# A convolution and an attention on one core: one pool of four PSUM tiles in the last quarter, in place of three tiles in turn

## The chip, the cores and the metric

The kernel runs on one core of one Trainium2 chip. The metric is device time in microseconds (us), the median of several executions. Engines are called as in the profile: PE (matmuls), PEld (PE's weight loads), DVE, ACT, POOL, and SP, which issues all the DMAs. PSUM is the memory that PE writes into and that DVE and ACT read; it holds eight tiles of 128 x 512 f32 here, one to a bank, and all eight are given away at any time.

## What is computed

Two independent results stand side by side in the output. Columns 0 to 447 are a long convolution of `A_u` (2048 x 448) with a kernel made from the `A_` parameters; columns 448 to 895 are attention with 16 heads of 28 over `B_x` (2048 x 448).

```python
K = 2.0 * jnp.einsum("dn,dnl->dl", C, exp((A * dt)[:, :, None] * pos)).real     # 448 x 2048, 256 terms each
a = irfft(rfft(u_t, 2 * L) * rfft(K, 2 * L), 2 * L)[:, :, :L] + u * D_skip
qkv = x @ wqkv
b = softmax(q k^T * Dh**-0.5) v, heads joined, @ wo
out = concatenate([a, b], axis=-1)
```

## The kernel before, in words

The first stage (lines 206 to 540) projects q, k and v, makes the seeds of the convolution's powers and the row maxima of the first unit of attention. Here the order on the engines is the planner's. From line 846 on every instruction keeps the order of the program on its engine, SP's DMAs too.

The main loop (lines 978 to 1030) has 256 steps. A unit `u` is a group of 4 heads and a chunk of 512 queries; it has 16 steps `kt`, one for each 128 keys. `ORDER` (line 33) is the order of a step: `m0 s0 m1 s1 v f pv f v m2 s2 m3 s3 v`.

- `s0` to `s3` are the scores of four heads (`s_mm`, line 698): a matmul into `pss` (a pool of three) and the exponential `p` on ACT. `pv` (line 705) multiplies the p of the step before by v, into `po`.
- `m0` to `m3` are the row maxima that a later unit will need, 19 steps ahead (`max_mm`, line 167). Each is a matmul into a working tile. For `m0` ACT reads the tile (`rl`, a Relu); for `m1` DVE's custom instruction joins it to that `rl`; for `m2` and `m3` DVE reduces it to `mx`. They end when 19 steps are left.
- `v` is a part of the convolution kernel's powers on DVE (`g`, with the factors in the PSUM tile `zg` of pool `ps_g`); POOL does another part (`e`).
- `f` calls `slot` (line 934), which runs the next small task that is due, if any: `sums`, `scale` and `project` of a finished unit (lines 726 to 753), the transform of u, the matmuls of the convolution kernel's blocks (`k_mm`), and then the jobs of the spectrum and of the output (`f_slot`).

A **spectrum job** (`spectrum`, line 760; 16 of them) has four tasks. `forth(0)` and `last` each run 8 matmuls `pm<-yk,mw` into a working tile (x16 in the trace, which counts two instructions for each), and DVE multiplies it by u's spectrum twice (`pr`, line 781). `last` then does both `join`s: DVE makes one half of `p0` and of `p1`, POOL the other (lines 786, 787). After a gap of two slots `back(0)` and `back(1)` run matmuls `pm<-p,mw` into a working tile each, and ACT copies it out (`y`). An **output job** (`finish`, line 803; 8 of them) has four tasks: matmuls `pm<-zi,wb`, and DVE adds `ut`, which POOL has multiplied (`ot`, line 836).

All these working tiles come from `w_tile` (line 124). It has three names, `pm0`, `pm1`, `pm2`, one tile each in pool `ps_m`, and takes them strictly in turn. A matmul that takes a tile waits until the tile's last reader has finished. So PSUM in the main loop is: `ps_m` 3, `pss` 3, `po` 1, `zg` 1.

The factors' tile `zg` is last needed when the convolution kernel's last block is done. Line 986 notes that point (step 192 or later, nothing left in `k_due`, `m_due`, `powers`), closes the pool of the blocks' SBUF tiles, and lets the second half of the spectrum jobs begin. In the trace the last use of `zg` lies at 1060 us and the last of the blocks' matmuls at 1076 us of the span, so line 986 acts at about 1079 us.

Of the kernel before, what the change touches and what calls it, by code (L numbers as in the profile page):

```python
# [7 lines left out]
F32 = mybir.dt.float32  # L8
# [5 lines left out]
PSUM = bass.MemoryType.PSUM  # L14
# [9 lines left out]
CQ = 512  # L24
# [64 lines left out]
def body(ctx, tc, a, out):  # L89
# [5 lines left out]
    def pool(stack, name, bufs=1, space=None, side=None):  # L95
        kw = {} if space is None else {"space": space}
        if side:
            kw["side"] = side
        return stack.enter_context(tc.tile_pool(name=name, bufs=bufs, reuse_waits="tile", **kw))
# [18 lines left out]
    w1 = const.tile([128, 2, 128], F32, name="w1")  # L118

    att, k0_st = ExitStack(), ExitStack()  # L120
    ps_m = pool(att, "ps_m", 1, PSUM)
    n_ring = [0]

    def w_tile():

        n_ring[0] += 1
        return ps_m.tile([128, CQ], F32, name=f"pm{n_ring[0] % 3}")

    q_p = pool(att, "q_p", side="right")
    v_p = pool(att, "v_p", side="right")  # L130
# [10 lines left out]
    def load_k(g, j, p):  # L141
        t = p.tile([128, L], F32R, name="khat", bufs=HG)
        for r in range(4):
            nc.sync.dma_start(t[32 * r:32 * r + 32, :].bitcast(F32), k_d[g][r % 2, 32 * j:32 * j + 32, :])
        kt_g.setdefault(g, []).append(t)
# [3 lines left out]
    def load_v(g, c):  # L149
        v_g[g, c] = t = v_p.tile([128, NK // NQ, HG, 32], F32, name="v", bufs=5)  # L150
        nc.sync.dma_start(t.rearrange("p t h e -> p t (h e)"), v_d[c][:, g])
# [3 lines left out]
    def load_kd(g, j):  # L155
        kd_g[g, j] = t = kd_p[0].tile([128, CQ], F32R, name=f"kdif{j}")
        for r in range(4):
            nc.sync.dma_start(t[32 * r:32 * r + 32].bitcast(F32), kd_d[g][r % 2, 32 * j:32 * j + 32, :])

    def load_q(u):  # L160
        g, c = divmod(u, NQ)
        t = q_p.tile([128, HG, CQ], F32R, name="qhat", bufs=3)
        for r in range(4):
            nc.sync.dma_start(t[32 * r:32 * r + 32].bitcast(F32), q_d[g][c][r // 2].rearrange("(j p) q -> p j q", j=HG))
        q_u[u] = t

    def max_mm(u, i, kc, ps=w_tile):

        if i == 0 and kc == 0:
            m_u[u] = q_p.tile([128, HG, 4, 3], F32, name="mx", bufs=2)  # L170
        j, t = divmod(i, 4)
        pm = ps()
        q, kt = q_u[u][:, j, t * 128:(t + 1) * 128], kt_g[u // NQ][j]
        mx = m_u[u][:, j, t, max(kc - 1, 0):max(kc - 1, 0) + 1]
        if kc == 0:
            nc.tensor.matmul(pm, q, kd_g[u // NQ, j], start=True, stop=True)
            rl_u[u, i] = kd_p[0].tile([128, CQ], F32, name="rl", bufs=2)
            nc.scalar.activation(rl_u[u, i], pm, AF.Relu)
        elif kc == 1:
            kb = kt.rearrange("p (c s n) -> p c s n", c=NQ, s=2)[:, :2, 1, :]  # L180
            nc.tensor.matmul(pm.rearrange("p (c n) -> p c n", c=2), q, kb, start=True, stop=True)
            rl = rl_u.pop((u, i))
            nc.vector.tensor_tensor_reduce(rl, pm, rl, 1.0, -3.0e38, ALU.add, ALU.max, mx)
        else:
            nc.tensor.matmul(pm, q, kt[:, kc * CQ:(kc + 1) * CQ], start=True, stop=True)
            nc.vector.tensor_reduce(mx, pm, axis=AX.X, op=ALU.max)
# [19 lines left out]
    with ExitStack() as st:  # L206
# [3 lines left out]
        x_p = pool(xst, "x_p")  # L210
        y_p = pool(wst, "y_p", side="right")
        w_p = pool(wst, "w_p", side="right")
        ps_t = pool(st, "ps_t", 2, PSUM)
        ps_n = pool(st, "ps_n", 2, PSUM)
        ps_x = pool(st, "ps_x", 1, PSUM)
# [223 lines left out]

        def qk_proj(c, s, g):  # L440
            pp = w_tile()
            hs = slice(HG * g, HG * g + HG)
            n = 0
# [99 lines left out]
    kq_st = ExitStack()  # L543
# [2 lines left out]
    g_p = pool(g_st, "g_p")  # L546
    ps_s = pool(att, "ps_s", 3, PSUM)
    ps_o = pool(att, "ps_o", 1, PSUM)
    ps_g = pool(att, "ps_g", 1, PSUM)
    k_pools = [k0_p, kq_p]  # L550

    late = [False]
# [145 lines left out]
    def s_mm(u, kt, j):  # L698
        pss = ps_s.tile([128, CQ], F32, name="pss")
        nc.tensor.matmul(pss, kt_g[u // NQ][j][:, kt * 128:(kt + 1) * 128], q_u[u][:, j, :], start=True, stop=True)  # L700
        p = kq_p.tile([128, CQ], F32, name="p", bufs=PB)
        nc.scalar.activation(p, pss, AF.Exp, scale=SCALE)
        return p

    def pv_step(u, kt, ps):
        if kt == 0:
            o_u[u] = ps_o.tile([128, CQ], F32, name="po")
        for j in range(HG):
            nc.tensor.matmul(o_u[u][32 * j:32 * j + 32, :], v_g[u // NQ, kt // NQ][:, kt % NQ, j, :], ps[j],
                             start=kt == 0, stop=kt == NK - 1, tile_position=(0, 32 * j))  # L710
# [3 lines left out]
    def load_og(u):  # L714
        og_u[u] = og = kq_p.tile([128, G - 1, CQ], F32, name="og")
        nc.sync.dma_start(og, on_d[u % NQ][:G - 1].rearrange("g p q -> p g q"))
# [169 lines left out]
    f0_st, f1_st = ExitStack(), ExitStack()  # L886
# [47 lines left out]
    def slot(s_):  # L934
        n_slot[0] += 1
        if urgent and urgent[0][0] <= n_slot[0]:
            urgent.popleft()[2]()
        elif s_ >= NS and f_slot(s_, "s"):
            pass
        elif p_due and p_due[0][0] <= s_:  # L940
            p_due.popleft()[1]()
        elif m_due and m_due[0][0] <= s_:
            m_due.popleft()[1]()
        elif u_due and u_due[0][0] <= s_:
            u_part(*u_due.popleft()[1:])
        else:
            f_slot(s_, "s") or f_slot(s_, "f")

    def k_begin(s_):
        if not (k_due and K0 + k_due[0] * KP <= s_ and done["mm"] >= k_due[0] - 2 and not powers["e"] and not powers["g"]):  # L950
            return
        b = k_due.popleft()
        k_start(b)
        powers["g"] += g_powers(b)
        powers["e"] += [lambda i=i, q=q: e_power(b, i, q) for i in range(3) for q in range(3)]
        p0, p1, p2 = k_mm(b)

        def m1():
            p1()
            done["mm"] = b  # L960
        m_due.extend((s_ + KD, t_) for t_ in (p0, m1, p2))
        last[0] = b
# [10 lines left out]
    def vec():  # L973
        if powers["g"]:
            powers["g"].popleft()()

    prev = None
    for s in range(NS):
        u, kt = divmod(s, NK)
        sm = s + NK + LEAD  # L980
        k_begin(s)
        if s == 12 * NK:
            k0_st.close()
            f_p["s", 0] = f_p["s", 1] = pool(f0_st, "f0_p", side="right")
            f_ready["s", 0], f_ready["s", 1] = s, NS
        if s >= 12 * NK and f_ready["s", 1] == NS and not (k_due or m_due or powers["g"] or powers["e"]):
            g_st.close()
            f_ready["s", 1] = s + F1
        if kt == 12 and u // NQ == G - 1:
            load_og(u)  # L990
        late[0] = s + NK + LEAD > NS
        if u % NQ == NQ - 1 and u < NU - 1 and kt % 4 == 2:
            load_v(u // NQ + 1, kt // 4)
        if sm < NS and sm // NK % NQ == NQ - 1 and sm % NK % 4 == 0 and sm % NK and sm // (NQ * NK) + 1 < G:
            load_kd(sm // (NQ * NK) + 1, sm % NK // 4 - 1)
        if sm < NS and sm % (NQ * NK) == 0 and sm:
            load_kd(sm // (NQ * NK), HG - 1)
        if kt % 4 == 1 and u % NQ == 1 and u // NQ + 1 < G:
            load_k(u // NQ + 1, kt // 4, k_pools[(u // NQ + 1) % 2])
        if kt == 2:  # L1000
            if u + 2 < NU:
                load_q(u + 2)
        for _ in range(3):
            if powers["e"]:
                powers["e"].popleft()()
        ps = []
        for op in ORDER:
            if op[0] == "s":
                ps.append(s_mm(u, kt, int(op[1])))
            elif op[0] == "f":  # L1010
                slot(s)
            elif op[0] == "v":
                vec()
            elif op == "pv":
                if prev:
                    pv_step(*prev)
                    if prev[1] == NK - 1:
                        fin(prev[0], s)
            elif sm < NS:
                max_mm(sm // NK, sm % NK, int(op[1]))  # L1020
        for _ in range(FX if late[0] else 0):
            slot(s)
        if sm < NS and sm % NK == NK - 1:
            def end(un=sm // NK):
                max_end(un, w_tile())
                max_put(un)
            max_join(sm // NK)
            soon_slot(UG[0], end)
        k_next()
        prev = (u, kt, ps)  # L1030
# [4 lines left out]
        slot(s)  # L1035
        s += 0.5
    assert not k_due and not powers["g"] and not powers["e"]
    for st in (f1_st, kq_st, f0_st, att):
        st.close()


# [55 lines left out]
```

## Time and profile before

| | us |
|---|---|
| median of 3 runs (1426.0 to 1428.26) | 1427.25 |
| the profiled execution | 1427.0 |
| its span, first to last instruction | 1425.2 |
| span from 1079.5 to 1341.5 (after line 986 acts, until the spectrum jobs are nearly done) | 262.0 |
| span from 1341.5 to 1404 (output jobs, attention without maxima) | 62.5 |
| span from 1404 to the end | 21.2 |

The profile and its trace are of one execution; the 1.8 us between its time and its span lie outside the instructions. PEclk is the clock that PE was granted, as a part of full speed. A row of the timeline gives start, length, engine, line, operation, out<-in, shapes and the number of instructions merged, and in brackets how long the engine sat idle before it, and for what. Line 73 is that of a helper which records every instruction, so tiles tell the groups apart, not lines. A matmul's length is modelled and overlaps the next one's start.

### The profile page before, as it was taken

The numbers are of one execution on the slowest core, as the hardware profiler recorded it, in microseconds if no ns is written. First come the engines' busy times: TensorE is split into PE (matmuls) and PEld (weight loads), VectorE is DVE, ScalarE is ACT, GpSimd is POOL, SyncE is SP. The second block draws the span as 40 slices with busy tenths as digits, with TensorE's granted clock in tenths as the row PEclk, the third lists the DMA queues.
The fourth block names the chain that finished last, engine by engine and source line by source line (L and its number), as shares of the span: only waits on it lengthen the run. The fifth ranks groups of instructions, "written<-read, shape, count | busy, mean of one in ns | idle before, by whom it ended". The sixth has DMA issues, their size and how long they took to land.

```text
span 1425.2 us, 33209 instructions
## 1 busy us (share of the span) xinstructions
PE 1273.5 (89%) x12625; PEld 707.7 (50%) x12625; DVE 978.6 (69%) x2138; ACT 974.4 (68%) x2069; POOL 830.8 (58%) x705
## 2 busy tenths in 40 slices
PE   6978856899999999999999999999988898898998
PEld 4756633445555555555555555555544444433433
DVE  5688766877778777777777878877786646645411
ACT  5867642688788888888787877878775545544553
POOL 3657650587778787778878878887861101102211
PEclk9998887899999999999999999999999999998999
DMA  6666679447663654586441316333244334435476
GB/s 190 236 235 216 225 267 249 112 98 180 150 149 85 152 151 122 157 200 165 140 91 40 92 36 150 89 79 84 55 136 134 112 106 144 154 110 164 134 199 175
DMA packets 200729, 205.37 MB, mean 144 GB/s; under 512 B 96632, under 2 KB 159160, under 8 KB 198520
## 3 DMA queue, kind: packets, MB, share of 16 engines
q1 hardware_dynamic: 200568, 203.23, 51.4%
q8 instruction: 100, 1.64, 0.5%
q14 instruction: 61, 0.50, 0.1%
HBM read 120.73 MB, written 82.18 MB: 142 GB/s over the span
## 4 chain that ended last, share of the span: by engine, by line
PE 58%; DVE 23%; ACT 7%; POOL 6%; issue 3%; DMA 3%; SPq 0%; ACTq 0%; DVEq 0%; POOLq 0%
PE pm L73 34%; PE po L73 13%; PE pss L73 11%; DVE mx L73 5%; DVE g L73 4%; DVE rl L73 3%; DVE p L73 3%; POOL qhat L73 3%; ACT p L73 2%; DVE pr L73 2%; ACT rl L73 2%; DVE tri L73 1%; DVE px L73 1%; DVE zg L73 1%; POOL x_e L73 1%
## 5 line engine op out<-in xcount | busy, mean ns | idle before, releaser
L73 ACT ACTIVATE p<-pss 128x512 f32<-128x512 f32 x1024 | 563.0, 607 | 162.4 <-PE pss L73 153.4
L73 DVE TENSOR_REDUCE mx<-pm 128x1 f32<-128x512 f32 x500 | 321.3, 683 | 141.5 <-PE pm L73 140.6
L73 PE MATMUL pss<-qhat,khat 128*128 128x512 f32 x1024 | 405.2, 402 | 3.2 <-ACT p L73 3.2
L73 PE MATMUL pm<-khat,qhat 128*128 128x512 f32 x749 | 335.3, 451 | 62.0 <-DVE mx L73 60.2
L73 POOL TENSOR_TENSOR e<-e,sdb 128x256 f32<-128x256 f32 x168 | 201.6, 1200 | 185.2 <-ACT e L73 129.6
L73 PE MATMUL po<-p,v 128*32 128x512 f32 x2048 | 278.8, 612 | 0.0
L73 PEld LDWEIGHTS pm<-khat,qhat 128*128 128x128 f32 x749 | 142.4, 190 | 247.3 <-DVE mx L73 114.9
L73 POOL TENSOR_TENSOR e<-e,eu 128x256 f32<-128x256 f32 x168 | 248.3, 1478 | 13.2
L73 DVE CUSTOM_DVE_ANT_0 rl<-pm,rl 128x512 f32<-128x512 f32 x249 | 171.5, 689 | 107.2 <-ACT rl L73 86.9
L73 PEld LDWEIGHTS pss<-qhat,khat 128*128 128x128 f32 x1024 | 192.0, 190 | 46.1 <-ACT p L73 12.8
L73 POOL TENSOR_TENSOR eu<-e,sdb 128x256 f32<-128x256 f32 x168 | 201.9, 1202 | 0.0
L73 POOL TENSOR_TENSOR p<-pr,pr 64x448 f32<-64x448 f32 x32 | 40.6, 1269 | 237.5 <-DVE pr L73 236.3
L73 ACT ACTIVATE rl<-pm 128x512 f32<-128x512 f32 x249 | 150.2, 603 | 32.3 <-PE pm L73 31.6
L73 DVE TENSOR_TENSOR g<-g,zg 128x128 f32<-128x128 f32 x392 | 162.7, 415 | 5.0
L73 PE MATMUL pm<-kdif,qhat 128*128 128x512 f32 x249 | 103.7, 417 | 14.9 <-DVE ot L73 4.0
L73 PEld LDWEIGHTS pm<-e,g 128*32 128x32 f32 x3584 | 64.0, 110 | 52.2 <-issue 34.2
L73 DVE TENSOR_TENSOR zg<-g,zg 128x128 f32<-128x128 f32 x224 | 87.3, 390 | 3.5
L73 ACT ACTIVATE y<-pm 128x448 f32<-128x448 f32 x48 | 26.3, 549 | 80.4 <-PE pm L73 54.1
L73 PEld LDWEIGHTS po<-p,v 128*32 128x32 f32 x2048 | 57.5, 111 | 43.8 <-issue 39.1
L73 PE MATMUL pm<-e,g 128*32 128x64 f32 x3584 | 72.8, 220 | 0.0
L73 PEld LDWEIGHTS pm<-kdif,qhat 128*128 128x128 f32 x249 | 47.3, 190 | 43.5 <-PE pss L73 9.7
L73 PE MATMUL pm<-xh,wh 112*128 112x512 f32 x128 | 54.5, 430 | 13.5 <-DVE tl L73 6.3
(137 smaller groups left out, 1545.8 us busy)
## 6 DMA issues: line engine op xcount, KB each, us to landing
sdb<-sd SPq DMA_DIRECT2D x56, 336.0 KB
qhat<-q SPq DMA_DIRECT2D x64, 256.0 KB
khat<-k SPq DMA_DIRECT2D x64, 256.0 KB
sd<-sg SPq DMA_DIRECT2D x8, 1456.0 KB
mw<-in_mw SPq DMA_DIRECT2D x16, 512.0 KB
sd<-qhat SPq DMA_DIRECT2D x8, 896.0 KB
yk<-yk SPq DMA_DIRECT2D x56, 128.0 KB
yu_d<-ub SPq DMA_DIRECT2D x64, 112.0 KB
```

What stands on the lines that cost most here:

```text
L73: i = f(*args, **kw)
```

## The change

`w_tile` now takes its pool and its number of names from `ps_w`. The three names of the first stage come from a pool `ps_w` that closes with that stage; the main loop gets a new pool `ps_m` with the same three names. When line 986's condition holds, `ps_g` and `ps_m` are closed and a pool `ps_f` is opened over their four banks. It has one name and four buffers; from there on a working tile is any of the four that the pool hands out, not the next in a fixed turn.

```diff
-    ps_m = pool(att, "ps_m", 1, PSUM)
-    n_ring = [0]
+    ps_w, n_ring = [None, 3], [0]
...
         n_ring[0] += 1
-        return ps_m.tile([128, CQ], F32, name=f"pm{n_ring[0] % 3}")
+        return ps_w[0].tile([128, CQ], F32, name=f"pm{n_ring[0] % ps_w[1]}")
...
+        ps_w[0] = pool(st, "ps_w", 1, PSUM)
...
-    ps_g = pool(att, "ps_g", 1, PSUM)
+    ps_st = ExitStack()
+    ps_g = pool(ps_st, "ps_g", 1, PSUM)
+    ps_w[0] = pool(ps_st, "ps_m", 1, PSUM)
...
             g_st.close()
+            ps_st.close()
+            ps_w[:] = pool(ps_st, "ps_f", 4, PSUM), 1
```

More of the change, by code (lines that the diff above doesn't have):

```diff
@@ L1037, in body @@
     assert not k_due and not powers["g"] and not powers["e"]
-    for st in (f1_st, kq_st, f0_st, att):
+    for st in (ps_st, f1_st, kq_st, f0_st, att):
         st.close()
```

## The prediction

> **What bounds the kernel now.** I looked first at where PE is busy and at what clock, because the change can act only after line 986: in the page's slices (PE and PEclk), then in a table by stage.
>
> ```profile
> PE   6978856899999999999999999999988898898998
> PEclk9998887899999999999999999999999999998999
> DMA  6666679447663654586441316333244334435476
> 1079.50:1341.50 262.00, 224.96 (x2044) 108.17 (x2042) 151.74 (x257) 128.43 (x244) 41.30 (x32) 0.92 0.42 137
> 1341.50:1404.00 62.50, 59.05 (x554) 22.32 (x554) 8.68 (x22) 36.13 (x69) 11.98 (x6) 1.00 0.71 189
> 1404.00:1425.20 21.20, 15.96 (x216) 6.65 (x216) 3.73 (x9) 2.38 (x5) 2.10 (x1) 0.98 0.50 135
> ```
>
> The columns of the table are the stretch and its length, then the busy time of PE, PEld, DVE, ACT and POOL, the granted clock, the DMA share and GB/s. In the 262 us after line 986 PE is busy 225 us, more than any other engine; it loses 37.0 us in idling and works at a clock of 0.92, so about 0.08 x 262 = 21 us more go in slow matmuls. Behind 1341.5 PE is nearly full at clock 1.00, and maxima and joins are over: little is to be had there. So at most some 58 us stand to be won. Next, the waits of PE in that stretch (total, times, longest):
>
> ```profile
> PE pm L73 <- DVE mx L73: 24.0, 10, 2.5
> PE pm L73 <- DVE ot L73: 5.0, 2, 4.0
> PE pm L73 <- DVE pr L73: 3.2, 13, 0.3
> PE pm L73 <- DVE mh L73: 2.4, 1, 2.4
> PE pm L73 <- DVE p L73: 1.5, 2, 0.9
> ```
>
> All but the last row are waits for a working tile that DVE hasn't read yet; the last is for an operand. Ten stalls of 2.4 us on the maxima carry it. The timeline of one such stall says why:
>
> ```profile
> 1196.06 0.94 PE L73 MATMUL pm<-yk,mw 128*32 128x224 f32 x16
> 1196.93 0.50 PE L73 MATMUL pm<-khat,qhat 128*128 128x512 f32 x1
> 1197.06 1.16 DVE L73 TENSOR_TENSOR pr<-pm,ub 128x448 f32<-128x448 f32 x2 [0.46 <-PE pm L73]
> 1197.49 0.39 PE L73 MATMUL pm<-khat,qhat 128*128 128x512 f32 x1
> 1198.25 2.67 DVE L73 TENSOR_TENSOR p<-pr,pr 64x448 f32<-64x448 f32 x2
> 1198.37 0.47 PE L73 MATMUL pm<-kdif,qhat 128*128 128x512 f32 x1 [0.26 <-DVE pr L73]
> 1198.68 0.40 PE L73 MATMUL pss<-qhat,khat 128*128 128x512 f32 x1
> 1198.87 0.60 ACT L73 ACTIVATE rl<-pm 128x512 f32<-128x512 f32 x1
> 1200.85 1.28 DVE L73 TENSOR_REDUCE mx<-pm 128x1 f32<-128x512 f32 x2
> 1201.58 0.50 PE L73 MATMUL pm<-khat,qhat 128*128 128x512 f32 x1 [2.51 <-DVE mx L73]
> 1201.92 0.40 PE L73 MATMUL pss<-qhat,khat 128*128 128x512 f32 x1
> 1202.25 1.85 PE L73 MATMUL po<-p,v 128*32 128x512 f32 x8
> 1203.85 1.74 PE L73 MATMUL pm<-p,mw 128*32 128x224 f32 x16
> ```
>
> `last` (1196.06) is followed on PE by m2 (1196.93) and m3 (1197.49), and on DVE by two `pr`, then both joins (2.67 us, needing no PSUM at all), and only then by the reduces of m2 and m3 (1200.85). The next step's m0 (1198.37) takes the tile of `last`; its m1 takes, by turn, the tile of m2, and stands until 1201.58. PE idles 2.51 us. Note the `rl` at 1198.87: ACT has read m0's tile by 1199.47, two microseconds before m1 gets its own, but the turn doesn't give that tile out.
>
> **The stall also closes the clock.** Slicing the span at the points where the clock changes gives steps of 3.41 us:
>
> ```profile
> 1065.86:1069.28 3.42, 1.94 (x22) 0.87 (x26) 2.72 (x5) 0.60 (x1) 0.34 (x1) 1.00 0.00 0
> 1103.41:1106.82 3.41, 1.77 (x22) 1.11 (x26) 2.88 (x5) 1.38 (x4) 0.50 (x1) 1.00 0.22 80
> 1106.82:1110.24 3.42, 3.42 (x32) 2.05 (x24) 1.43 (x3) 2.20 (x5) 0.00 (x0) 1.00 0.30 100
> 1117.06:1120.48 3.42, 1.26 (x5) 0.48 (x3) 3.31 (x4) 1.87 (x4) 1.57 (x2) 1.00 0.00 0
> 1120.48:1123.89 3.41, 3.41 (x29) 1.52 (x32) 0.70 (x2) 1.14 (x2) 0.00 (x0) 0.50 0.04 13
> ```
>
> A step in which PE idles 3.42 - 1.26 = 2.16 us is followed by one at half clock (1117.06, then 0.50 at 1120.48); a step with 3.41 - 1.77 = 1.64 us idle (1103.41) is not (1106.82, at 1.00). So here the point lies between 1.64 and 2.16 us of idling inside one step. What a half-clock step costs, from two stretches with the same work (m1, s1, back, pv, back, up to m2), one without it and one with it:
>
> ```profile
> 1105.05 0.50 PE L73 MATMUL pm<-khat,qhat 128*128 128x512 f32 x1 [2.15 <-DVE mx L73]
> 1108.25 0.50 PE L73 MATMUL pm<-khat,qhat 128*128 128x512 f32 x1
> 1119.85 0.50 PE L73 MATMUL pm<-khat,qhat 128*128 128x512 f32 x1 [2.15 <-DVE mx L73]
> 1124.67 0.50 PE L73 MATMUL pm<-khat,qhat 128*128 128x512 f32 x1
> ```
>
> 3.20 us against 4.82 us: 1.62 us each. The 21 us above are thus 13 such steps.
>
> **The change, part by part.** It adds no instruction and takes none away; every engine keeps its order, and SP's DMAs theirs. The first stage keeps three names and the main loop starts with three, in other banks; the first maxima of the main loop find banks that nobody uses, so nothing is queued there, and I cost that part at nothing (both ends within 1 us: the largest wait it could move is one reduce, 0.64 us of the 1.28 us row). The switch itself gives out banks whose readers finished long ago (`zg`) or one step ago: at most the two reduces of one step, 1.28 us, once; I take nothing.
>
> What is left is which tile a matmul waits for. Four tiles in a fixed turn would move the wait on m2's reduce by one tile, from m1 to `back(0)`. But a pool with several buffers doesn't take turns: it gives out whichever comes free first in the planner's order. The built program of the kernel before shows it in its two-tile pool `ps_t`, in the maxima of the first unit: three times a tile read by ACT's `rl` alone is given out again at once, while the other, waiting for a DVE reduce, is passed over. So `back(0)` should get m0's tile, free after the `rl`.
>
> Worked on the stall above, where PE takes 0.34 us for a full-width matmul after a halt (1201.58 to 1201.92) and 0.22 to 0.23 for the next (1196.93 to 1197.49 is 0.56 for both), 0.86 for a pv, and the first join 1.20, both by the chain that ended last:
>
> ```profile
> 1195.38 0.86 PE po L73 x8
> 1198.25 1.20 DVE p L73
> ```
>
> m0 would start at 1197.94, m1 at 1198.40 (it gets the tile of `last`, whose `pr` ends at 1198.22), s1, pv at 1198.96, `back(0)` at 1199.82. Its operand p0 is the first join, done at 1198.25 + 1.20 = 1199.45. It ends at 1200.9. Now m2 needs a tile: m2's old one at about 1201.5 (the end of the first of the two reduces), or that of `back(0)` after ACT's copy, about the same. **What is late next is thus m2, by some 0.65 us**, in place of 2.51. Where a small task stands between m1 and pv (three of the ten) it takes m0's tile in the same way, and the wait left is no longer in sum; I take the same. That is seven stalls of this form: 7 x (2.5 - 0.65) = 13.0 us.
>
> The other three of the ten have `last` ahead of pv, and the stall comes a step later:
>
> ```profile
> 1184.94 0.40 PE L73 MATMUL pss<-qhat,khat 128*128 128x512 f32 x1
> 1185.48 0.60 ACT L73 ACTIVATE rl<-pm 128x512 f32<-128x512 f32 x1
> 1187.48 0.50 PE L73 MATMUL pm<-khat,qhat 128*128 128x512 f32 x1 [2.14 <-DVE mx L73]
> ```
>
> There m1 and s1 run on at 1185.2, `back(0)` wants its tile at 1185.73 and gets m0's at 1186.08: 0.3 us are left, and pv then covers the reduce. 3 x (2.15 - 0.3) = 5.5 us.
>
> The small waits on `pr` (3.2 us, 13 times) fall with the fourth tile, since m0 needn't take the tile just multiplied: 3.0 us. At the one stall on `mh` the tiles of `last`, `mh`, m2 and m3 are all behind the joins; only m0 and its `rl` get ahead: 2.4 becomes 1.8, 0.6 us. At the 4.0 us stall on `ot` DVE itself waits for POOL, behind POOL's share of the joins; two matmuls get ahead, 0.8 us; the other `ot` wait goes whole, 1.0 us.
>
> Sum of the idling: 13.0 + 5.5 + 3.0 + 0.6 + 0.8 + 1.0 = 24 us of the 37.
>
> With single waits of 0.3 and 0.65 us no step idles 1.64 us any more, so the clock stays open, but for the `ot` stall and perhaps the `mh` one: two half-clock steps of 13 stay. 11 x 1.62 = 18 us.
>
> Hidden cost: DVE must now do its work in 262 - 42 = 220 us; it is busy 152 us there, ACT 128, and both wait on PE after each stall today. The DMA share of 0.42 becomes 0.5; the page's first seven slices stand at 0.6 to 0.9. The next job's loads are issued one job ahead. I count nothing for these.
>
> 1427.0 - 24 - 18 = **1385 us** for the profiled execution; it stands 0.25 us under the median, which I leave out.
>
> **The bounds.** If every wait but those on an operand went and the clock stayed open: 37.0 - 1.5 + 21 = 56.5 us, 1370.5. From the other side, see the rivals.
>
> **The rivals.** (1) *The turn stays.* If the planner gives the four out as a ring, `back(0)` waits for m2's reduce. In the seven-stall form without a small task (four) that leaves 1201.58 - 1200.0 = 1.58 us, counting m1, s1 and pv run meanwhile as won; PE then reaches `back(0)` 1.54 us sooner (0.34 + 0.34 + 0.86). In the three others of that form, and in the form with `last` ahead of pv, only m1 and s1 get ahead, 0.68 us each. 4 x 1.54 + 6 x 0.68 + 2 for the rest = 12 us; seven of the stalls are then near 1.6 us, about the longest that left the clock open: 7 x 1.62 = 11 us. 1427 - 23 = 1404. For it: a plan is not the chip. Against it: m0's `rl` is done 2 us ahead of m2's reduce in the trace, a wide margin for a plan to miss.
>
> (2) *The clock closes all the same*, since a job still has several short waits in one step: 1427 - 24 = 1403. Against it: steps with 1.48 us idle (1065.86, row above) and 1.64 us stayed open. [...]
>
> (3) *The stall only moves*, since DVE's joins stay in front of the reduces: each stall saves what one score matmul and one maximum cover, 0.46 us, 12 x 0.46 = 6, and some of the clock, 5: 1416.
>
> (4) *No change:* another thing ends last in every job, and the won time is given back at the next wait. [...] Here 35 us of waits carry the name of a PSUM tile, which speaks against it.
>
> (5) *Slower:* the plan misjudges the joins and gives m0, not m1, the tile whose reduce lies behind them. Then m0 and s0 lose the cover that they have today, 0.56 us at each of 12 stalls: 1427 + 6.7 = 1434. It decides if the plan has DVE through 2.67 us of joins and one reduce within the 0.7 us that PE takes from m2 to m0. That is unlikely.
>
> **Chances.** Forecast 1385: 0.50. Rivals 1 and 2 together, 1403 to 1404: 0.27. Rival 3, 1416: 0.10. No change: 0.06. Slower, 1434: 0.07. The range reaches down to that bound and the rivals 1 and 2 with some margin: 1371 to 1414. A difference under 0.2% (2.9 us) can't be told from none. Faster 0.87, same 0.06, slower 0.07.
>
> **What would show it.** In the profile after: PEclk of 0.98 to 1.00 in the stage behind line 986; PE's waits on `mx` from 24 us to below 9; m1 at most 0.3 us behind m0's pair after each join; DVE's and ACT's busy times as before. If instead `back(0)` waits for `mx` for 1.6 us, rival 1 holds; if the idling falls and the clock doesn't rise, rival 2. I am wrong altogether if PE waits at m0, or if a wait on a DMA or on ACT takes the place of the one on `mx`.

## The result and the profile after

The changed kernel takes 1383.35 us (median of 4, 1381.05 to 1385.67) against 1426.62 for the kernel before beside it (median of 4, 1424.25 to 1428.26): a ratio of 0.9698, 95% interval 0.9682 to 0.9714, or 43 us less. The profiled execution has a span of 1381.8 us, 43.4 less than before.

These are the rows of PE and of its clock on the page in 40 slices, of the kernel after:

```profile
PE   6977874899999999999999998999999999998997
PEclk9989996899999999999999999999999999999999
```

From slice 31 on the clock stands at 9 throughout, where before it had one 8: a tenth is too coarse. PE's row, which had an 8 in six of these ten slices, has one, and a 7 at the very end. The table by stage says more. Its stretches are the same pieces of work as those of the kernel before (each ends at the same matmuls), and its columns are the same: the stretch and its length, the busy time of PE, PEld, DVE, ACT and POOL, the granted clock, the DMA share and GB/s.

```profile
1081.60:1298.30 216.70, 201.57 (x2044) 104.51 (x2042) 150.27 (x257) 125.70 (x244) 41.61 (x32) 0.99 0.51 166
1298.30:1360.70 62.40, 59.05 (x554) 22.35 (x554) 8.67 (x22) 36.04 (x69) 11.92 (x6) 1.00 0.71 191
1360.70:1381.80 21.10, 15.76 (x216) 6.79 (x216) 3.72 (x9) 2.42 (x5) 2.11 (x1) 1.00 0.48 129
```

The stage behind line 986 shrank from 262.0 to 216.7 us, with the same numbers of matmuls (x2044) and nearly the same busy time on DVE, ACT and POOL. The other two stretches did not move. Of the 45.3 us, PE's idling gave 37.0 - 15.1 = 21.9 and PE's busy time 225.0 - 201.6 = 23.4, at a clock of 0.99 in place of 0.92. What PE still waits for in that stretch (total, times, longest):

```profile
PE pm L73 <- DVE mx L73: 4.7, 6, 0.9
PE pm L73 <- DVE ot L73: 3.5, 1, 3.5
PE pm L73 <- ACT rl L73: 1.9, 4, 0.8
PE pm L73 <- DVE p L73: 1.5, 2, 0.9
```

The 24.0 us on `mx` have become 4.7, and there is no row for `pr` any more. The timeline of the first pair of joins behind line 986 shows the new order of waits:

```profile
1083.71 0.94 PE L73 MATMUL pm<-yk,mw 128*32 128x224 f32 x16
1085.61 0.40 PE L73 MATMUL pm<-kdif,qhat 128*128 128x512 f32 x1
1085.91 2.69 DVE L73 TENSOR_TENSOR p<-pr,pr 64x448 f32<-64x448 f32 x2
1086.08 0.41 PE L73 MATMUL pm<-khat,qhat 128*128 128x512 f32 x1
1086.38 0.61 ACT L73 ACTIVATE rl<-pm 128x512 f32<-128x512 f32 x1
1086.66 1.07 PE L73 MATMUL po<-p,v 128*32 128x512 f32 x8
1087.54 0.94 PE L73 MATMUL pm<-p,mw 128*32 128x224 f32 x16
1088.53 1.27 DVE L73 TENSOR_REDUCE mx<-pm 128x1 f32<-128x512 f32 x2
1089.26 0.50 PE L73 MATMUL pm<-khat,qhat 128*128 128x512 f32 x1 [0.78 <-DVE mx L73]
```

m1 (1086.08) runs right behind m0's pair, and `back(0)` (1087.54) runs a microsecond ahead of the reduce that it would have had to wait for in a fixed turn. What is late next is m2, by 0.78 us. One long stall is left, at the output job's `ot`; there the clock closes once:

```profile
1190.70:1194.12 3.42, 1.87 (x20) 0.94 (x22) 3.37 (x6) 2.25 (x5) 1.49 (x2) 1.00 0.81 269
1248.73:1252.14 3.41, 1.03 (x10) 0.59 (x14) 1.48 (x3) 0.37 (x2) 1.90 (x1) 1.00 0.86 202
1252.14:1255.56 3.42, 3.42 (x35) 1.44 (x28) 0.71 (x3) 0.87 (x2) 0.00 (x0) 0.50 0.20 67
```

In this trace, from 290 us on, the clock changes only at the ends of steps of 3.41 us. The step with 3.41 - 1.03 = 2.38 us idle is followed by one at 0.50. Of the other steps in this stage the one that idled most, 3.42 - 1.87 = 1.55 us, is not.

### The profile page after: what moved, and what is told of

Its sections match the earlier page's. It is cut to its first block, busy times and chain, and to the rows that moved or that the text cites. A ratio compares the mean times of both kernels' runs of the same rounds, so it can differ in the third digit from the quotient of the medians.

```text
span 1381.8 us, 33199 instructions
## 1 busy us (share of the span) xinstructions
PE 1254.3 (91%) x12625; PEld 707.4 (51%) x12625; DVE 979.4 (71%) x2138; ACT 971.6 (70%) x2069; POOL 830.7 (60%) x705
## 3 DMA queue, kind: packets, MB, share of 16 engines
q8 instruction: 100, 1.64, 0.5%
## 4 chain that ended last, share of the span: by engine, by line
PE 58%; DVE 23%; ACT 7%; POOL 5%; issue 3%; DMA 2%; SPq 0%; ACTq 0%; DVEq 0%; POOLq 0%
PE pm L73 34%; PE po L73 13%; PE pss L73 11%; DVE mx L73 6%; DVE g L73 4%; DVE rl L73 3%; POOL qhat L73 3%; ACT p L73 2%; DVE p L73 2%; ACT rl L73 2%; DVE tri L73 1%; DVE pr L73 1%; DVE px L73 1%; DVE sg L73 1%; DVE zg L73 1%
## 5 line engine op out<-in xcount | busy, mean ns | idle before, releaser
L73 PE MATMUL pm<-khat,qhat 128*128 128x512 f32 x749 | 333.9, 449 | 45.3 <-DVE mx L73 39.6
L73 POOL TENSOR_TENSOR e<-e,sdb 128x256 f32<-128x256 f32 x168 | 201.6, 1200 | 185.5 <-ACT e L73 129.7
L73 PE MATMUL po<-p,v 128*32 128x512 f32 x2048 | 272.2, 599 | 0.0
L73 PEld LDWEIGHTS pss<-qhat,khat 128*128 128x128 f32 x1024 | 191.3, 189 | 47.2 <-ACT p L73 12.9
```

The costliest lines, as they stand in the source:

```text
L73: i = f(*args, **kw)
```

## The experiments

The theory: the gain comes from two things, one more tile and the hand-out of whichever tile is free first, which together keep PE going past DVE's joins; and about half of the gain is the clock, which the long stalls had been closing. The rivals: only the number of tiles counts; the low clock costs nothing of its own; the joins have no special part in it; or the new pools at the start of the main loop have a share.

**Four tiles in turn** (the changed kernel, edited).

```diff
-            ps_w[:] = pool(ps_st, "ps_f", 4, PSUM), 1
+            ps_w[:] = pool(ps_st, "ps_f", 1, PSUM), 4
```

> The four tiles of the changed kernel, but with four names taken strictly in turn instead of one pool of four. Theory (which tile is handed out matters as much as how many there are): back(0) waits for the reduce behind the joins, as in rival 1 of the prediction; PE's longest waits on mx stay near 1.6 us and the time is 1404 us, between 1397 and 1410. Rival (only the number of tiles matters): the same as the changed kernel, 1383 us within 3.

Measured: 1400.03 us (1398.25 to 1400.97), ratio to before 0.9814, interval 0.9795 to 0.9832. So 26 us come with a fourth tile even in turn, and 17 more with free hand-out. The stage behind line 986, PE's waits in it, and two pairs of neighbouring steps of the clock:

```profile
1081.92:1315.63 233.71, 205.70 (x2043) 106.40 (x2042) 150.76 (x256) 125.21 (x243) 41.50 (x32) 0.97 0.47 153
PE pm L73 <- DVE mx L73: 19.7, 11, 2.5
```

```profile
1126.37:1129.78 3.41, 1.16 (x43) 0.60 (x47) 3.36 (x5) 0.97 (x2) 1.11 (x1) 1.00 0.02 6
1129.78:1133.20 3.42, 3.42 (x24) 2.18 (x17) 1.05 (x5) 1.62 (x3) 0.00 (x0) 0.50 0.04 12
1174.16:1177.57 3.41, 1.63 (x8) 1.00 (x7) 3.40 (x4) 2.56 (x5) 2.11 (x2) 1.00 0.24 99
1177.57:1180.98 3.41, 3.41 (x44) 2.18 (x45) 1.51 (x4) 1.16 (x3) 0.00 (x0) 1.00 0.20 67
```

The waits on `mx` fall only from 24.0 to 19.7 us and the idling from 37.0 to 28.0, yet 26 us are won, because PE's busy time falls from 225.0 to 205.7. Here a step with 1.78 us idle leaves the clock open and one with 2.25 closes it. Most stalls are now of the first kind: 4 half-clock steps are left of 13.

**Three tiles, handed out freely.**

```diff
-            ps_w[:] = pool(ps_st, "ps_f", 4, PSUM), 1
+            ps_w[:] = pool(ps_st, "ps_f", 3, PSUM), 1
```

> The changed kernel, but its last pool has three tiles, so the factors' bank lies unused: free hand-out without the fourth tile. Theory: after a join m1 waits only for ACT's rl of m0 (about 0.5 us) and back(0) for the reduce (about 0.6 us); no step of the clock idles over 1.6 us, so most half-clock steps go, and the time is 1393 to 1402 us. Rival (only the number of tiles matters): three tiles are three tiles, 1422 us or more.

Measured: 1405.4 us (1401.65 to 1408.17), ratio 0.9854, interval 0.9831 to 0.9876. The rival is out: with no tile more, 20 us are won. The time lies 3 us above the upper end of the theory's range. The rows show where:

```profile
PE pm L73 <- DVE mx L73: 7.9, 10, 1.3
PE pm L73 <- ACT rl L73: 5.7, 11, 0.8
PE pm L73 <- DVE pr L73: 3.2, 13, 0.3
PE pm L73 <- DVE mh L73: 2.4, 1, 2.4
```

The waits on ACT's `rl` are in m1, as expected (in ten of the eleven cases, 0.45 to 0.80 us each). Those on `pr` and `mh` stay whole, and those on `ot` too (5.3 us, where 5.0 were). The clock was misjudged as well: over the whole run it is 0.968, where it was 0.961 before and 0.973 after, and a half-clock step stays even behind a step that idled only 1.67 us. The last section comes back to this.

**Matmuls without use in the stall** (the kernel before, edited; three tiles in turn). The added product is read by nobody; the flag is set after each pair of joins behind line 986. (The rows say L74, since the added constant moves the helper down by a line.)

```diff
+NFILL = 5
...
+    def filler(u, kt):
+        fill[0] = False
+        z = ps_g.tile([128, CQ], F32, name="zg")
+        for _ in range(NFILL):
+            nc.tensor.matmul(z, kt_g[u // NQ][0][:, kt * 128:(kt + 1) * 128], q_u[u][:, 0, :], start=True, stop=True)
...
             join(0)
             join(1)
+            fill[0] = late_on[0]
...
             g_st.close()
+            late_on[0] = True
...
             elif sm < NS:
+                if op == "m1" and fill[0]:
+                    filler(u, kt)
                 max_mm(sm // NK, sm % NK, int(op[1]))
```

> The kernel before, with three tiles in turn, and five matmuls without use put on PE ahead of the first m1 after each pair of joins, into the factors' bank, which is idle by then; their product is not read. They take 5 x 0.23 = 1.15 us of a stall of 2.2 to 2.5 us, so they lie inside it. Theory (idling over about 1.64 us in a step closes the clock): the ten stalls on mx leave 1.0 to 1.4 us idle, their 10 half-clock steps go, 10 x 1.62 = 16 us are saved with no tile won, and the time is 1410 us, between 1406 and 1414; the granted clock of the stage rises from 0.92 to 0.98. Rival (the low clock costs nothing beside the waits): 1427 us, or up to 1438 if the added matmuls are paid in full.

Measured: 1412.7 us (1411.51 to 1414.44), ratio 0.9907, interval 0.9891 to 0.9924. A kernel that does more work, and gets no tile sooner, is 13 us shorter. One stall of it:

```profile
1127.63 0.47 PE L74 MATMUL pm<-kdif,qhat 128*128 128x512 f32 x1 [0.25 <-DVE pr L74]
1128.17 1.33 PE L74 MATMUL zg<-qhat,khat 128*128 128x512 f32 x5
1130.87 0.50 PE L74 MATMUL pm<-khat,qhat 128*128 128x512 f32 x1 [1.37 <-DVE mx L74]
```

m1 still waits for `mx`, but PE idles 1.37 us in place of 2.5. The stage behind line 986, in the table's columns:

```profile
1080.80:1327.80 247.00, 221.25 (x2104) 115.56 (x2102) 151.81 (x257) 128.66 (x244) 41.67 (x32) 0.99 0.45 146
```

The clock there is 0.99 in place of 0.92, and 2 half-clock steps are left of 13. So the low clock is shown to cost time of its own. The 13 us are what is left after two deductions. Ten of the twelve groups lie inside stalls on `mx`; the other two come behind the stalls on `mh` and `ot`, which are in m0, and PE pays them in full, at half clock. One of the two:

```profile
1209.81 2.22 PE L74 MATMUL zg<-qhat,khat 128*128 128x512 f32 x5
```

The next matmul starts at 1211.86, so this group takes 2.05 us, and the one behind `ot` (1277.10 to 1279.23) 2.13 us. And ahead of line 986 one more step closes than in the kernel before (at 1068.40). The stage alone is 15 us shorter; with the 4 us of the two groups the clock's share in it is an estimated 19 us, for 11 half-clock steps.

**The joins off DVE** (the kernel before, edited; three tiles in turn).

```diff
-            nc.vector.tensor_tensor(t_["p", e][:64], t_[0, 0][es], t_[1, 1][es], ALU.subtract)
+            nc.gpsimd.tensor_tensor(t_["p", e][:64], t_[0, 0][es], t_[1, 1][es], ALU.subtract)
```

> The kernel before, with DVE's halves of the joins put on POOL too, so that DVE goes from pr straight to the reduces; POOL's part of a job doubles to about 5.1 us. Theory (DVE's joins ahead of the reduces are what PE stalls on): the waits on mx of 2.2 to 2.5 us go with three tiles in turn, back(0) waits up to 1 us for POOL, the clock stays open, and the time is 1388 to 1400 us. Rival (three tiles are too few whatever DVE does): 1420 us or more.

Measured: 1392.41 us (1391.03 to 1394.94), ratio 0.9766, interval 0.9748 to 0.9784. PE's longest waits behind line 986:

```profile
PE pm L73 <- POOL p L73: 11.4, 16, 2.1
PE pm L73 <- DVE ot L73: 6.4, 1, 6.4
```

No wait on `mx` is left in that list. The stall was made by DVE's order (joins ahead of reduces); a fourth tile is one way past it, less work on DVE ahead of the reduces another. POOL takes its price: where up to 1 us was expected, PE waits for its `p` up to 2.1 us, and the stall on `ot`, for which DVE itself waits on POOL's `ut` (7.06 us), grows from 4.0 to 6.4 us.

**Everything but the switch.**

```diff
             g_st.close()
-            ps_st.close()
-            ps_w[:] = pool(ps_st, "ps_f", 4, PSUM), 1
```

> The changed kernel without the switch: the pools of the first stage and of the main loop as changed (other banks), but three tiles in turn to the end. Theory (all of the gain lies behind line 986): the time before, 1426 us within 2. Rival (new banks at the start of the main loop save waits there): 1420 us or less.

Measured: 1426.82 us against 1426.94 beside it, ratio 0.9999, interval 0.999 to 1.0008. The other banks and pools are worth nothing that can be measured.

**Free hand-out in the main loop too.**

```diff
-    ps_w[0] = pool(ps_st, "ps_m", 1, PSUM)
+    ps_w[:] = pool(ps_st, "ps_m", 3, PSUM), 1
```

> The changed kernel, with the main loop's three tiles too as one pool of three, handed out freely, and the pool of four behind line 986. In the main loop PE waits 35 us for mx, in 49 waits of 0.2 to 1.2 us, where DVE's powers lie ahead of the reduces; the rl of the last m0 ends only 0.2 us before the reduce that PE waits for, so theory expects a fifth of it, 7 us: 1376 us, between 1368 and 1384. Rival (free hand-out wins as much there as behind line 986, where two thirds of the waiting went): 1360 us. A third view, that a plan for three tiles is wrong as often as right: 1384 us or more.

Measured: 1395.09 us (1393.86 to 1396.26), ratio to before 0.9778, interval 0.9764 to 0.9792: 12 us slower than the changed kernel. The third view was right and the theory wrong. PE's waits from 290 to 1076 us of the span, first of the changed kernel, then of this one:

```profile
PE pm L73 <- DVE mx L73: 35.1, 49, 2.5
```

```profile
PE pm L73 <- ACT rl L73: 42.7, 57, 1.5
PE pm L73 <- DVE mx L73: 3.8, 13, 0.5
```

And the same stretch in the table by stage, of the one and of the other:

```profile
290.00:1076.00 786.00, 747.21 (x8777) 409.64 (x8776) 603.77 (x1428) 629.83 (x1405) 626.20 (x491) 1.00 0.47 118
```

```profile
290.00:1076.00 786.00, 734.64 (x8613) 400.37 (x8605) 594.48 (x1410) 623.61 (x1385) 622.82 (x488) 1.00 0.47 115
```

The pool gives m1 the tile that ACT's `rl` frees, and does away with the waits on `mx`; but in the main loop ACT too is behind, with the scores' exponentials ahead of each `rl`, and 42.7 us of new waits are more than the 31 saved. Over these 786 us PE's busy time falls from 747.2 to 734.6, so that the same work takes some 12 us longer. One of these waits:

```profile
698.13 1.08 ACT L73 ACTIVATE p<-pss 128x512 f32<-128x512 f32 x2
698.58 1.28 DVE L73 TENSOR_REDUCE mx<-pm 128x1 f32<-128x512 f32 x2
699.11 0.60 ACT L73 ACTIVATE rl<-pm 128x512 f32<-128x512 f32 x1
699.76 0.50 PE L73 MATMUL pm<-khat,qhat 128*128 128x512 f32 x1 [0.80 <-ACT rl L73]
```

The first of the two reduces ends at about 699.2 and frees a tile, the `rl` only at 699.71; m1 still waits for the `rl`. So m1 did not get the tile that came free first on the chip, but the one that the plan had given it.

**The second join off DVE** (the changed kernel, edited).

```diff
-            nc.vector.tensor_tensor(t_["p", e][:64], t_[0, 0][es], t_[1, 1][es], ALU.subtract)
+            (nc.gpsimd if e else nc.vector).tensor_tensor(t_["p", e][:64], t_[0, 0][es], t_[1, 1][es], ALU.subtract)
```

> The changed kernel, with DVE's half of the second join on POOL; DVE keeps its half of the first, which back(0) needs. The reduces behind the joins come 1.45 us sooner, so the 0.75 us waits left at m2 (some 10 of them) go; back(1) finds p1 from POOL about as it comes to it. Theory: 15 us of idling in the stage become 8, and the time is 1376 us, between 1372 and 1380. Rival (POOL's longer part, about 3.8 us a job, stops back(1) and the ut multiplication): 1383 us or more.

Measured: 1370.73 us (1369.63 to 1371.81), ratio 0.9607, interval 0.9593 to 0.9621, the shortest of all. The stage behind line 986 of this kernel, and PE's waits in it:

```profile
1076.04:1284.68 208.64, 199.88 (x2041) 104.23 (x2043) 127.84 (x242) 126.24 (x246) 56.76 (x46) 0.99 0.53 172
```

```profile
PE pm L73 <- DVE ot L73: 2.9, 1, 2.9
PE pm L73 <- ACT rl L73: 1.7, 4, 0.8
PE pm L73 <- DVE mx L73: 0.9, 3, 0.3
PE pm L73 <- POOL p L73: 0.5, 1, 0.5
```

The waits on `mx` are 0.9 us, and POOL's longer part costs 0.5 us. PE idles 8.8 of 208.6 us, near the 8 expected. The time is 5 us below the one expected and 1 us below the range. The expectation counted only the stage: there 216.7 became 208.6, and another 5 us of the span were won ahead of line 986, where the first spectrum job's joins stall PE as well (1.04 us in place of 2.50).

**Both of these edits together.**

> The two edits of the other runs of this call together: the main loop's three tiles handed out freely, and the second join on POOL. They act in different stretches, so their gains should add: 1369 us, between 1361 and 1377. If they don't add, the time is that of the better of the two.

Measured: 1385.96 us (1385.03 to 1390.5), ratio 0.972, interval 0.9703 to 0.9737, above the expected range, which had counted on a gain from the first edit. The gain of one and the loss of the other add within 4 us: 1370.7 + (1395.1 - 1383.4) = 1382.4.

## Why the prediction was right, point by point

- **Where and what bounds.** Right. All of the gain is behind line 986 (without the switch the ratio is 0.9999), and moving the joins by themselves takes the stalls on `mx` away.
- **Which tile is handed out.** Right, and it carries 17 us: in turn 1400.0, freely 1383.4. Of these, 28.0 - 15.1 = 12.9 us are idling. Rival 1 had put the turn at 1404, with 12 us less idling and 11 from the clock; it was 9 us less idling, and more from the clock, since nine half-clock steps went and not seven.
- **What is late next.** m2, by 0.78 us where 0.65 was expected. That holds where no small task stands between; where one does, the waits were taken as the same and are not always: at 1122.68 a small task waits 0.47 us for `rl`, and at 1124.73 `back(0)` 0.71 us for `mx`.
- **The idling**, 24 us expected, 21.9 measured. The waits on `pr` went whole, as expected. In the three stalls that have `last` ahead of pv, `back(0)` waits 0.38 us where 0.3 was expected. The profile names no releaser for these, but each ends 0.1 us behind m0's `rl`, as in the first two rows below. The term for `ot` was too large twice. Of the 4.0 us stall 0.8 was to go, and it became 3.5, because the pool gave m1 the very tile that waits for `ot`. And the 1.0 us at the other `ot` was to go whole; it came back behind the next pv as a wait for the operand `m`, the third row: there the stall only moved, as rival 3 had it for all of them.

```profile
1099.58 0.60 ACT L73 ACTIVATE rl<-pm 128x512 f32<-128x512 f32 x1
1100.28 0.96 PE L73 MATMUL pm<-p,mw 128*32 128x224 f32 x16 [0.38 <-issue]
1279.73 0.27 PE L73 MATMUL pm<-ident,m 128*16 128x128 f32 x1 [1.04 <-DVE m L73]
```

- **The clock**, 18 us expected, about 19 by the count: 12 of 13 half-clock steps went, one more than expected, at 1.62 us. The condition it went by, a point between 1.64 and 2.16 us of idling in a step, held here (1.55 us left the clock open, 2.38 closed it), but the point is not sharp (last section). PE's busy time fell by 23.4 us. The 4 us between are not settled by a run. By the prediction's own rows a full-width matmul takes 0.34 us after a halt and 0.23 without one, and there are fewer halts, which goes the same way.
- **What luck took.** The one long stall ahead of line 986, 2.50 us in both and unchanged by the edit, closed the clock in the profiled execution after. In the one before it did not, because there it straddled two steps, at 1062.45 with 1.27 us idle and at 1065.86 with 1.48. The last matmuls of the convolution kernel's blocks start at 1075.72 us before and at 1077.84 after, which is most of the reason why 45 us in the stage became 43 in the span. That the sum of 42 us met the 43 measured is partly luck too: the idling gave 2 us less than forecast, PE's busy time 5 us more than the 18 forecast for the clock, and 2 us were lost here. The steps after:

```profile
1064.41:1067.82 3.41, 0.73 (x3) 0.30 (x2) 3.36 (x5) 1.83 (x4) 2.27 (x2) 1.00 0.43 173
1067.82:1071.24 3.42, 3.35 (x18) 1.21 (x22) 1.31 (x4) 0.60 (x1) 0.00 (x0) 0.50 0.00 0
```

- **Rival 5** (a plan that misjudges who is free first) didn't happen behind line 986. Something like it did happen in the main loop when the pool there was handed out freely too, with ACT, not DVE, as the engine misjudged.

## What to carry to other kernels

Where PE stops for a working tile, look at what the reader does ahead of reading it: a block on DVE that needs no PSUM, put ahead of the reads, held PE for 2.1 to 2.5 us in most jobs, and moving half of that block to an engine with time to spare gave 13 us on top of the tile change's 43. A free pool helped here only as far as the planned order of release was the chip's; it won 17 to 20 us behind line 986 and lost 12 us in the main loop, where ACT ran late. And count a stall's price with the clock: here filling ten stalls with matmuls without use, which freed no tile sooner, took 13 us off the whole.

## What the runs showed of the hardware

In the traces before and after, from 290 us on, the granted clock is 1.00 or 0.50 and changes only at the ends of steps of 3.41 us. Thirteen steps at full clock (11 before, 2 after) idled 1.98 to 3.41 us, and each was followed by a step at half clock. All others at full clock idled 1.64 us or less, and none was. The edited kernels add two cases between: 1.78 us left the clock open with four tiles in turn (1174.16), while 1.67 us closed it with three handed out freely (1279.19, below). So the idling that the rows show gives no sharp point.

```profile
1279.19:1282.61 3.42, 1.75 (x6) 0.59 (x4) 3.37 (x4) 2.72 (x5) 2.55 (x2) 1.00 0.38 150
1282.61:1286.02 3.41, 3.04 (x24) 1.19 (x28) 1.91 (x5) 0.00 (x0) 0.00 (x0) 0.50 0.02 5
```

A possible reason, an estimate from rows of these traces and not tested: the row of a full-width matmul is 0.40 us long, though the next one starts 0.23 us behind it (after, at 1120.75 and 1120.98), so each halt may be 0.17 us longer than the rows show. The step at 1279.19 holds three halts, the one at 1174.16 a single one. With 0.17 us added for each, the first comes to an estimated 1.67 + 0.51 = 2.18 us and the second to 1.78 + 0.17 = 1.95, in the order that the clock showed. In the kernel before, two half-clock steps were followed by a second one though they idled less, at 1086.34 with 0.78 us and at 1287.73 with 0.55.

So matmuls whose product nobody reads made the kernel 13 us shorter. Whether one stall closes the clock depends on where it falls among the steps: the same 2.50 us stall did in the execution after and did not in the one before.
